# Moving the index load in front of the weights, re-ordering the start, and cutting loads and the last column finer, in a fused spectral-filter and gated-MLP kernel

## The chip, the cores and the metric

The kernel runs on one core of a Trainium2 chip. The time is that of one execution on the device, in microseconds (us); a profile gives a "span", which is about 1.7 us shorter than the time of the same execution (178.5 against 180.2 us). All executions below are with a granted TensorE clock of 0.996 to 1.0.

Engine names as in the profile: PE is TensorE (matmul), PEld its weight loads, DVE is VectorE, ACT is ScalarE, POOL is GpSimd, SP is the engine that issues the transfers (SPq: its queue).

## The reference, cut to what matters

```python
xn = _layernorm(x)                       # x: 2048 x 512, per row
A  = irfft2(rfft2(xn) * (w_r + 1j*w_i))  # spectral filter over both axes
g, u = xn @ w_gate, xn @ w_up            # 512 -> 1792
B  = (gelu(g) * u) @ w_down              # 1792 -> 512
return x + A + B
```

The 2048 rows are cut into 16 "columns" of 128 rows. A unit is a group of columns times some of the 14 blocks of 128 hidden features: its gate product goes through gelu on ACT (`ge`), DVE multiplies it with the up product (`hT`).

## The kernel before

The kernel records every operation with an estimated duration, and a planner orders them engine by engine. The order is fixed when the kernel is built; each engine then works through its list in turn. So a wrong estimate is not mended at run time: an engine stands in front of its next instruction until that one can start (1.66 us in one case below). The parts that matter here:

```python
# loads, all on one queue, in this order
load_x(0, 1)
load_x(1, 1)
for f0, f1 in ((0, 512), (512, 1024)):
    load_w(Wg_sb, f0, f1)
    load_w(Wu_sb, f0, f1)
    if f0 == 0:
        load_x(2, 2)
load_x(4, 4)
# ... third weight part, x 8-11, RF, x 12-15, constants ...
idx_t = pc.tile([P, 3], I32, name="idx_t")     # 128 rows of 12 bytes
nc.sync.dma_start(out=idx_t[:], in_=nc.inline_tensor(idx_np, name="spec_rows").ap())

# columns 2 and 3: moments, rsqrt in eight small DVE steps, normalise, transpose on PE, copy back
def second_two():
    m = [moments(c, -1200 + c) for c in (2, 3)]
    steps = rsqrt_steps(V, 2, 2)
    m = [add("DVE", 1.5, lambda: [f() for f in steps], m, key=-1190)]
    for c in (2, 3):
        xn_op[c] = add("DVE", 0.33, lambda c=c: f_norm_v(c, 0, D), m, key=-1180 + c, lat=0.53)
        # ... transpose and copy ...

# the first units: (first column, columns, first feature block, blocks)
todo = [(0, 1, 0, 2), (0, 1, 2, 2), (1, 1, 0, 4), (0, 2, 4, 2), (0, 2, 6, 2)]

# forward transform, four groups; each takes all four PSUM buffers "S" that ACT then copies out
def forward(cg, kv):
    # ...
    for q in range(4):
        m = pe(0.224, lambda q=q: mm(q), [f], 10 * cg + q, acq=("S",), rel=("xf",) if q == 3 else ())
        m.t_min = RF_LAND
        bs_ops.append(add("ACT", 0.5, lambda q=q: out(q), [m], key=10 + cg + 0.1 * q, rel=("S",)))

# output of column c; the last column in two halves
w = D if c < NC - 1 else D // 2
for o in range(0, D, w):
    # ... 14 matmuls, one more, DVE add, store ...
```

Between the warm-up matmuls and the first gate matmul PE runs six filler matmuls (`spin_on`), meant to keep its clock up.

## Time and profile before

| | before |
|---|---|
| time | 180.41 us, median of 3 (180.31 to 180.52) |
| span of the profiled execution | 178.5 us |
| PE busy | 172.8 us (97%) |
| DVE / ACT / POOL busy | 117.0 / 95.9 / 19.6 us |
| first gate matmul | 6.78 us |
| PE idle between that and the last matmul | 0.20 + 0.38 + 0.37 us |

First the head of the page: the span, PE's busy line and its strip of 40 slices.

```profile
span 178.5 us, 3086 instructions
...
PE   7999999999999999999999999999999999999992
```

PE is full everywhere but in the first and the last slice, so only the start, a few holes too short for the strip, and the tail can give time. The timeline of PE shows the start. Columns: start, length, engine, source line, operation, output and inputs, shape, count; in brackets the idle time in front and who ended it.

```profile
5.87 1.07 PE L318 MATMUL sp_ps<-x_t,spin 128*128 128x256 bf16 x6
6.78 0.61 PE L495 MATMUL g_ps<-xnT,Wg_sb 128*128 128x128 bf16 x8
...
8.10 1.07 PE L495 MATMUL u_ps<-xnT,Wu_sb 128*128 128x128 bf16 x16
9.00 1.06 PE L495 MATMUL g_ps<-xnT,Wg_sb 128*128 128x128 bf16 x16
10.27 1.05 PE L495 MATMUL g_ps<-xnT,Wg_sb 128*128 128x256 bf16 x8 [0.21 <-DMA Wg_sb<-in_B_w_gate_dram]
11.15 1.06 PE L495 MATMUL u_ps<-xnT,Wu_sb 128*128 128x128 bf16 x16
...
15.14 0.61 PE L495 MATMUL g_ps<-xnT,Wg_sb 128*128 128x256 bf16 x4
```

The eight matmuls at 10.27 need the second part of the gate weights, which landed at 10.22; the block before it issued its last matmul at 9.84 and the next could have started 0.05 later, so the hole is 0.38 us from start to start (the bracket counts from a modelled end). At 15.14 the first unit of columns 2 and 3 begins; this instant, called "gate block 2-3" below, closes the head, since PE runs without a wait from there to 40 us.

The one hole further on is in the forward transform. These are PE's timeline lines of the second and the third group:

```profile
35.98 1.06 PE L565 MATMUL bp<-RF_t,xf 128*128 128x128 bf16 x16
39.47 1.42 PE L565 MATMUL bp<-RF_t,xf 128*128 128x128 bf16 x16
```

And these are ACT's timeline lines between them; `Bs` are the copies out of PSUM, the memory that PE writes to; they free the buffers:

```profile
37.22 0.81 ACT L458 ACTIVATE xn<-x_t,nb,rstd 128x512 bf16<-128x512 bf16 x1 [1.66 <-POOL nb L373]
37.94 0.57 ACT L500 ACTIVATE ge<-g_ps 128x512 bf16<-128x512 f32 x1
38.42 2.04 ACT L535 CAST Bs<-bp 128x512 bf16<-128x512 f32 x4
```

Both groups on PE are 16 matmuls, but the second takes 1.42 us instead of 1.06: its tiles wait for these buffers. ACT could have copied out the group of 35.98 from about 36.4 on, but it stood 1.66 us in front of a normalisation that waited for POOL, and the copies came after it. The hole on PE is 0.37 us.

The tail, in DVE's timeline: the last add, after which only the store is left.

```profile
175.17 0.42 DVE L811 TENSOR_TENSOR y_sb<-y_ps,y_sb 128x256 bf16<-128x256 f32 x1 [0.73 <-PE y_ps L808]
```

### The profile page before, as it was taken

The page shows a single profiled execution, that of the slowest core. Times are in us where ns is not written, and L with a number is a line of the kernel's source. Part 1 is how long each engine was busy: PE and PEld are TensorE (multiplying, and loading weights), DVE is VectorE, ACT ScalarE, POOL GpSimd, SP SyncE. Part 2 cuts the span into 40 slices and gives each one's busy share as a digit, 9 for nine tenths or more (in the row PEclk, how much of TensorE's full clock was granted, in tenths as well). Part 3 has the DMA queues.
Part 4 walks back from the last instruction along what each step waited for, and adds up shares of the span by engine and source line. Part 5 has one row for each costly group of instructions (what it writes and reads, how often), then busy time and mean ns, then how long its engine had stood idle before and what let it go on. Part 6 is the DMA issues. An engine that isn't in the chain of part 4 may idle for free.

```text
span 178.5 us, 3086 instructions
## 1 busy us (share of the span) xinstructions
PE 172.8 (97%) x1100; PEld 95.7 (54%) x1118; DVE 117.0 (66%) x261; ACT 95.9 (54%) x172; POOL 19.6 (11%) x60
## 2 busy tenths in 40 slices
PE   7999999999999999999999999999999999999992
PEld 5688845464455544555555454454454445445461
DVE  3498999983843599979899999643616425334341
ACT  4633487969675988898899964362112112111200
POOL 1000363620576000000000000000000000000000
PEclk9999999999999999999999999999999999999999
DMA  4999944333392662211201520200122212222211
GB/s 117 350 384 393 371 130 95 79 63 32 70 296 106 217 200 59 56 26 37 54 23 44 130 69 15 59 0 0 62 88 88 90 59 62 90 87 63 84 33 59
DMA packets 21008, 19.36 MB, mean 108 GB/s; under 512 B 8128, under 2 KB 19520, under 8 KB 20992
## 3 DMA queue, kind: packets, MB, share of 16 engines
q1 hardware_dynamic: 20576, 17.84, 33.9%
q0 software_dynamic: 416, 1.32, 2.3%
q8 instruction: 9, 0.15, 0.3%
q14 instruction: 7, 0.06, 0.1%
HBM read 13.38 MB, written 2.10 MB: 87 GB/s over the span
## 4 chain that ended last, share of the span: by engine, by line
PE 90%; DMA 4%; ACT 2%; SPq 1%; issue 1%; DVE 1%
PE y_ps L804 27%; PE u_ps L495 26%; PE g_ps L495 25%; DMA Wg_sb<-in_B_w_gate_dram 4%; PE yp L756 2%; PE gp L726 2%; PE dp L623 2%; PE y_ps L808 2%; PE ep L632 2%; PE bp L565 1%; ACT Bs L535 1%; SPq L271 1%; ACT ge L500 1%; SPq L275 1%; DVE hT L505 0%
## 5 line engine op out<-in xcount | busy, mean ns | idle before, releaser
L495 PE MATMUL g_ps<-xnT,Wg_sb 128*128 128x512 bf16 (+2 forms) x268 | 57.1, 341 | 0.5 <-DMA Wg_sb<-in_B_w_gate_dram 0.2
L495 PE MATMUL u_ps<-xnT,Wu_sb 128*128 128x512 bf16 (+2 forms) x264 | 56.4, 340 | 0.3
L505 DVE TENSOR_TENSOR hT<-u_ps,ge 128x512 bf16<-128x512 f32 (+1 forms) x57 | 38.6, 678 | 19.3 <-PE u_ps L495 12.3
L804 PE MATMUL y_ps<-Wd_sb,hT 128*128 128x512 bf16 (+1 forms) x232 | 50.5, 366 | 0.3
L500 ACT ACTIVATE ge<-g_ps 128x512 bf16<-128x512 f32 (+1 forms) x57 | 34.1, 598 | 24.4 <-PE g_ps L495 23.0
L495 PEld LDWEIGHTS <-Wg_sb 128*128 128x128 bf16 x272 | 24.9, 98 | 21.5 <-DMA Wg_sb<-in_B_w_gate_dram 0.4
L495 PEld LDWEIGHTS <-Wu_sb 128*128 128x128 bf16 x272 | 24.8, 98 | 20.7 <-DMA Wu_sb<-in_B_w_up_dram 0.2
L804 PEld LDWEIGHTS <-hT 128*128 128x128 bf16 x238 | 22.9, 98 | 22.6
L762 ACT CAST yf<-yp 128x512 bf16<-128x512 f32 x16 | 9.3, 586 | 40.5 <-PE yp L756 40.5
L811 DVE TENSOR_TENSOR y_sb<-y_ps,y_sb 128x512 bf16<-128x512 f32 (+1 forms) x17 | 11.0, 659 | 30.2 <-PE y_ps L808 30.2
L637 ACT CAST E<-ep 64x512 bf16<-64x512 f32 x32 | 18.5, 578 | 0.9 <-PE ep L632 0.5
L333 DVE BATCH_NORM_STATS2 stats<-x_t 128x6 f32<-128x512 bf16 x16 | 10.4, 677 | 4.2 <-DMA x_t<-in_A_x_dram 4.0
L458 ACT ACTIVATE xn<-x_t,nb,rstd 128x512 bf16<-128x512 bf16 x12 | 9.8, 834 | 2.8 <-POOL nb L373 2.8
L535 ACT CAST ds<-dp 128x512 bf16<-128x512 f32 x16 | 9.2, 597 | 0.6 <-PE dp L623 0.5
L535 ACT CAST Gs<-gp 128x512 bf16<-128x512 f32 x16 | 8.7, 591 | 0.6 <-PE gp L726 0.5
L535 ACT CAST Bs<-bp 128x512 bf16<-128x512 f32 x16 | 8.5, 611 | 0.0
L768 DVE TENSOR_TENSOR lv<-yf 128x512 bf16<-128x512 bf16 x16 | 6.1, 421 | 1.5 <-ACT yf L762 0.7
L756 PEld LDWEIGHTS <-Gs 128*128 128x128 bf16 x64 | 4.8, 98 | 3.5
L775 DVE TENSOR_TENSOR yt<-lv 128x512 bf16<-128x512 bf16 x16 | 6.1, 421 | 0.3
L756 PE MATMUL yp<-CT,Gs 128*128 128x128 bf16 x64 | 6.0, 219 | 0.1
L808 PE MATMUL y_ps<-yt,RI_t 128*128 128x512 bf16 (+1 forms) x17 | 5.9, 366 | 0.0
L632 PE MATMUL ep<-ds,CT 128*128 128x512 bf16 x16 | 5.9, 379 | 0.0
(72 smaller groups left out, 121.5 us busy)
## 6 DMA issues: line engine op xcount, KB each, us to landing
F<-F SPq DMA_DIRECT2D x32, 64.0 KB, 2.0
y_sb<-in_A_x_dram SPq DMA_DIRECT2D x16, 128.0 KB, 2.1
out_dram<-y_sb SPq DMA_DIRECT2D x15, 128.0 KB, 1.7
Wd_sb<-in_B_w_down_dram SPq DMA_DIRECT2D x1, 1792.0 KB, 7.6
x_t<-in_A_x_dram SPq DMA_DIRECT2D x3, 512.0 KB, 11.5
Wg_sb<-in_B_w_gate_dram SPq DMA_DIRECT2D x2, 512.0 KB, 5.9
Wu_sb<-in_B_w_up_dram SPq DMA_DIRECT2D x2, 512.0 KB, 6.9
Wg_sb<-in_B_w_gate_dram SPq DMA_DIRECT2D x1, 768.0 KB, 9.4
```

The costliest lines, as they stand in the source:

```text
L333: V.bn_stats(out=st[:], in_=x_t[:, c, :])
L458: xn_op[c] = add("ACT", 0.72, lambda c=c: A.activation(out=xn[:, c, :], in_=x_t[:, c, :], func=AF.Identity, bias=nb[:, c:c + 1], scale=rst ...
L495: T_.matmul(b[name][:, f], lhsT=W_[:, e, (f0 + f) * P:(f0 + f + 1) * P], rhs=rhs[:, e, :], start=(e == 0), stop=(e == NE - 1))
L500: A.activation(out=b["ge"][:], in_=b["g_ps"][:], func=AF.Gelu_apprx_tanh)
L505: V.tensor_tensor(out=hT_of(sb, f0, m, o, w), in0=b["u_ps"][:], in1=b["ge"][:], op=ALU.mult)
L535: A.copy(out=o, in_=i)
L632: T_.matmul(t[:], lhsT=cc("L" if g + h else "L0"), rhs=b["ds", h][:], start=True, stop=True)
L637: A.copy(out=b["E"][64 * h:64 * h + 64, r], in_=b["ep", h][64 * r:64 * r + 64])
L756: T_.matmul(t[:, q], lhsT=late["G"][:, q, c0 + j], rhs=IQ[q], start=(q == 0), stop=(q == 3), skip_group_check=True)
L804: T_.matmul(b[o][:], lhsT=hT_of(sb, f, 1, cl * P, P)[:, 0], rhs=Wd_sb[:, f, o:o + w], start=(f == 0), stop=False)
L808: T_.matmul(b[o][:], lhsT=late["RI"][:, c, :], rhs=late["yt"][:, c, o:o + w], start=False, stop=True)
L811: V.tensor_tensor(out=b["y"][:, o:o + w], in0=b[o][:], in1=b["y"][:, o:o + w], op=ALU.add)
```

## The change

Its intent, as the code tells it: let column 1 land without weights behind it, order the start so that PE meets the loads later than they land, keep the small rsqrt steps of columns 2-3 together, shorten the last add and store. The diff, cut to its core (renamed variables and unchanged context left out):

```diff
     load_x(1, 1)
-    for f0, f1 in ((0, 512), (512, 1024)):
-        load_w(Wg_sb, f0, f1)
-        load_w(Wu_sb, f0, f1)
-        if f0 == 0:
-            load_x(2, 2)
-    load_x(4, 4)
+    idx_t = pc.tile([P, 3], I32, name="idx_t")
+    nc.sync.dma_start(out=idx_t[:], in_=nc.inline_tensor(idx_np, name="spec_rows").ap())
+    load_w(Wg_sb, 0, 512)
+    load_w(Wu_sb, 0, 512)
+    load_x(2, 2)
+    load_w(Wg_sb, 512, 1024)
+    load_w(Wu_sb, 512, 1024)
+    load_x(4, 2)
+    load_x(6, 2)
     ...                                  # x 8-11 and 12-15, RF and the constants in two each
-    LAND = {0: 2.9, 1: 3.8, 2: 7.9, 3: 7.9}
+    LAND = {0: 2.9, 1: 3.5, 2: 8.8, 3: 8.8}
-    WG_LAND = [5.6] * 4 + [9.3] * 4 + [15.0] * 6
-    WU_LAND = [7.0] * 4 + [10.8] * 4 + [17.0] * 6
+    WG_LAND = [6.6] * 4 + [10.2] * 4 + [15.0] * 6
+    WU_LAND = [8.0] * 4 + [11.7] * 4 + [17.0] * 6
     ...
         stats(1)
-        mean(1)
         recip(0)
         xn_(0, 0)
+        mean(1)
         xn_(0, 1)
-        recip(1)
     ...                                  # recip(1) after column 0's copies
+        hold[0] = m[0]                   # hT of unit 0 not before the rsqrt steps
+            hold[1] = xn_op[c]           # hT of unit 1 not before the normalisation
     ...
+        u = split("u_ps", "U", Wu_sb, 1000.5 + k, WU_LAND, 1 if k == 2 else m)
-    todo = [(0, 1, 0, 2), (0, 1, 2, 2), (1, 1, 0, 4), (0, 2, 4, 2), (0, 2, 6, 2)]
+    todo = [(0, 1, 0, 4), (1, 1, 0, 4), (0, 2, 4, 2), (0, 2, 6, 2)]
     ...
-        w = D if c < NC - 1 else D // 2
-        for o in range(0, D, w):
+        for o, w in ((0, D),) if c < NC - 1 else ((0, 256), (256, 128), (384, 128)):
```

`LAND` and its kin are the planner's estimates of when a load has landed; changing them changes the order, not the loads. On the queue five loads are cut in two, and the last store is.

More of the change, by code (lines that the diff above doesn't have):

```diff
@@ L280 @@
     load_x(1, 1)
-    for f0, f1 in ((0, 512), (512, 1024)):
-        load_w(Wg_sb, f0, f1)
-        load_w(Wu_sb, f0, f1)
-        if f0 == 0:
-            load_x(2, 2)
-    load_x(4, 4)
+    idx_t = pc.tile([P, 3], I32, name="idx_t")
[7 more added lines that the diff above has]
+    load_x(6, 2)
     load_w(Wg_sb, 1024, DF)
     load_w(Wu_sb, 1024, DF)
-    load_x(8, 4)
-    nc.sync.dma_start(out=RF_t[:], in_=rf_d.rearrange("p (c k) -> p c k", c=NC))
-    load_x(12, 4)
-    load_consts("F0", "M0")
-    LAND = {0: 2.9, 1: 3.8, 2: 7.9, 3: 7.9}
+    load_x(8, 2)
+    load_x(10, 2)
+    for c in range(0, NC, 8):
+        nc.sync.dma_start(out=RF_t[:, c:c + 8], in_=rf_d.rearrange("p (c k) -> p c k", c=NC)[:, c:c + 8])
+    load_x(12, 2)
+    load_x(14, 2)
+    load_consts("F0", "L0")
+    load_consts("I0", "M0")
+    LAND = {0: 2.9, 1: 3.5, 2: 8.8, 3: 8.8}
     LAND.update({c: 12.6 if c < 8 else 18.5 if c < 12 else 21.5 for c in range(4, NC)})
-    WG_LAND = [5.6] * 4 + [9.3] * 4 + [15.0] * 6
-    WU_LAND = [7.0] * 4 + [10.8] * 4 + [17.0] * 6
+    WG_LAND = [6.6] * 4 + [10.2] * 4 + [15.0] * 6
+    WU_LAND = [8.0] * 4 + [11.7] * 4 + [17.0] * 6
     RF_LAND = 20.0
-    idx_t = pc.tile([P, 3], I32, name="idx_t")
-    nc.sync.dma_start(out=idx_t[:], in_=nc.inline_tensor(idx_np, name="spec_rows").ap())
     for T, w_in in ((TR, A_w_r), (TI, A_w_i)):
@@ L427, in first_two @@
         copy(0, 1)
+        recip(1)
         v("xn1", lambda: f_norm_v(1, 0, D), 0.33, [("rstd", 1)], lat=0.45)
@@ L438, in moments @@
         return add("DVE", 0.1, lambda: f_mean(c), [s], key=key - 0.5)
+    hold = {}
     def second_two():
@@ L489, in unit, with mm @@
         rhs = xnT[sb][:, :, c0 % 4:c0 % 4 + n, :].rearrange("p e c q -> p e (c q)")
-        def mm(name, tag, W_):
-            b[name] = ps.tile([P, m, w], F32, name=name, tag=tag, bufs=2)
-            for f in range(m):
+        def mm(name, tag, W_, fs=range(m)):
+            if fs[0] == 0:
+                b[name] = ps.tile([P, m, w], F32, name=name, tag=tag, bufs=2)
+            for f in fs:
                 for e in range(NE):
@@ L508, in unit, with split @@
         src = [xT_op[c] for c in range(c0, c0 + n)]
-        g = add("PE", occ, lambda: mm("g_ps", "G", Wg_sb), src, key=1000 + k, lat=occ + 0.3, acq=("G",),
-                t_min=WG_LAND[f0 + m - 1])
-        u = add("PE", occ, lambda: mm("u_ps", "U", Wu_sb), src, key=1000.5 + k, lat=occ + 0.3, acq=("U",),
-                t_min=WU_LAND[f0 + m - 1])
+        def split(name, tag, W_, key, t, h):
+            o = None
+            for f in range(0, m, h):
+                o = add("PE", occ * h / m, lambda f=f: mm(name, tag, W_, range(f, f + h)), [o] if f else src, key=key,
+                        lat=occ * h / m + 0.3, acq=() if f else (tag,), t_min=t[f0 + f + h - 1])
+            return o
+        g = split("g_ps", "G", Wg_sb, 1000 + k, WG_LAND, 2 if k == 0 else m)
+        u = split("u_ps", "U", Wu_sb, 1000.5 + k, WU_LAND, 1 if k == 2 else m)
         ge = add("ACT", {1: 0.28, 2: 0.36, 4: 0.5}[n * m], f_ge, [g], key=-1000 + k,
                  lat={1: 0.38, 2: 0.48, 4: 0.7}[n * m], acq=("ge",), rel=("G",))
-        h = add("DVE", {1: 0.21, 2: 0.34, 4: 0.61}[n * m], f_h, [ge, u], key=-1000 + k, rel=("U", "ge"))
+        h = add("DVE", {1: 0.21, 2: 0.34, 4: 0.61}[n * m], f_h, [ge, u], key=-1000 + k, rel=("U", "ge"),
+                after=hold.get(k))
         for c in range(c0, c0 + n):
@@ L816, in down @@
         x = add("SP", 0.36, load, key=1000 + c, lat=2.6, acq=("y_sb",), t_min=100.0)
-        w = D if c < NC - 1 else D // 2
-        for o in range(0, D, w):
+        for o, w in ((0, D),) if c < NC - 1 else ((0, 256), (256, 128), (384, 128)):
             k = 2000 + 10 * c + o / D
-            m = add("PE", 14 * w * 0.000421, lambda o=o: mm(o, w), [h_op[c, f] for f in range(NFC)] + [wd],
+            m = add("PE", 14 * w * 0.000421, lambda o=o, w=w: mm(o, w), [h_op[c, f] for f in range(NFC)] + [wd],
                     key=k, acq=("S",))
-            r = add("PE", w * 0.000421, lambda o=o: ri_mm(o, w), [m, yt_op[c], ri], key=k + 0.1,
+            r = add("PE", w * 0.000421, lambda o=o, w=w: ri_mm(o, w), [m, yt_op[c], ri], key=k + 0.1,
                     lat=w * 0.000421 + 0.3)
             m.lat = m.occ
-            t = add("DVE", 0.1 + w * 0.001, lambda o=o: total(o, w), [r, x], key=k, rel=("S",))
-            add("SP", 0.36, lambda o=o: store(o, w), [t], key=k, lat=2.0, rel=("y_sb",) if o + w == D else ())
+            t = add("DVE", 0.1 + w * 0.001, lambda o=o, w=w: total(o, w), [r, x], key=k, rel=("S",))
+            add("SP", 0.36, lambda o=o, w=w: store(o, w), [t], key=k, lat=2.0, rel=("y_sb",) if o + w == D else ())
     for c in range(NC):
```

## The prediction

> **What bounds it now.** TensorE. In the timeline, matmuls follow each other without a gap from 10.27 us to 175.1 us of the 178.5 us span (PE busy 97%, granted clock 1.0 throughout). The only holes after the first gate matmul at 6.78 us: 0.20 us before 8.10 (first up weights), 0.38 before 10.27 (the chain of waits blames the second gate load, issued 3.27, landed 10.22), and 0.37 inside the third forward-transform group (40.0 to 40.5), whose PSUM buffers ScalarE freed late because it sat 1.66 us in order behind GpSimd (37.22). About 0.95 us in all. After the last matmul: VectorE add 0.42, store 1.6 to landing, 1.3 to the end. Only the head, these holes and the tail can give anything; no matmul column is removed.
>
> **What the change does.**
> 1. The index load goes in front of the weights. Its issue takes 0.33 us (timeline), plus about 0.05. Column 1 then has a tiny transfer, not 512 KB of weights, behind it: landed at 4.00, it should land near 3.5. The weights are issued about 0.37 later, and I expect loads to land 0.2 to 0.4 later: first gate 6.64 to about 6.95, up 8.05 to 8.35, columns 2-3 8.74 to 9.05, second gate 10.22 to 10.5.
> 2. Column 0's chain shortens (column 1's mean moved behind): copies end near 6.0 instead of 6.4. That buys nothing: the first gate matmul waits for weights, near 7.0 instead of 6.78.
> 3. Column 1's 16 up matmuls (0.87 us) now come before the second gate block, so the 0.38 us hole closes.
> 4. The rsqrt steps of columns 2-3 run unbroken (about 1.6 us), but the first hT multiply (0.69) sits between them and the normalisation. I reckon stats 9.1, scale 12.2, xn 12.9 to 13.6: PE may wait 0.2 to 0.4 us at the third up tile and the transposes. The gate block of columns 2-3, at 15.14 now, starts between 14.8 and 15.4: head worth -0.3 to +0.3 us.
> 5. Split loads move the same bytes; the queue is bandwidth-bound at 360 to 415 GB/s until about 22 us: nothing on the critical path.
> 6. Re-planned order: the second and third forward groups move about 2 units back, so the 0.37 us hole probably closes.
> 7. Tail: from adds of 0.69 (512 columns) and 0.42 (256) I estimate 0.29 for 128, saving 0.13 us. PE time is equal (128-wide matmuls already run at 54 ns). The Trainium skill, "DMA: Bandwidth & Descriptors" (Anatomy of one DMA), puts the fixed part near 2.0 us; here whole stores take 1.7 and halves 1.6, so halving again gains 0 to 0.05. The same page (Specifications) says transfers below 512 B are not line-rate, and these rows are 256 B: a small risk of the opposite sign. No run here shows it yet.
>
> **Sum.** Head about 0, forward hole -0.3, tail -0.15: from 180.41 to **180.0 us**, 8 in 10 between **179.3 and 180.7**. Faster by over 2%: 0.01; within 2%: 0.98; slower by over 2%: 0.01.
>
> **What would show it.** Column 1 landing near 3.5; first gate matmul near 7.0, no wait for the second gate load; gate block of columns 2-3 at 15.1 +- 0.3; no stall over 0.1 us in the forward groups; last add near 0.29 us, last store landing in about 1.6.
>
> **What would make it wrong.** The index load not delaying the weights (0.3 more gain); its 12-byte rows blocking queues longer than one issue (loss); a new in-order stall of ScalarE behind GpSimd or the late table load; 256-byte stores landing slower than 2 us.

## The result, and the profile after

The change took the time from 180.45 us (180.31 to 180.52) to 179.38 us (179.14 to 179.73), four runs each. The ratio is 0.9943, 95% interval 0.9922 to 0.9964. Ratios here are the mean time of one kernel's runs over that of the other's of the same rounds, so not quite the ratio of the medians quoted. A second series, of five runs (whether on the same chip is not on record), gave 179.21 us against 179.81 for before, ratio 0.9971 (0.9958 to 0.9984). The gain is thus 0.5 to 1.1 us. The two series differ mainly in the kernel before: all its four runs of the first series lie above 180.3 us, and the profiled execution (180.2) had late loads (below). Why it was slower there is not shown. The forecast of 180.0, range 179.3 to 180.7, held the result near its lower edge.

First the head of the page again, span and PE's strip:

```profile
span 177.5 us, 3118 instructions
...
PE   7999999998999999999999999999999999999993
```

The 8 in the tenth slice (40 to 44 us) is the larger hole shown below.

PE's timeline at the start, to be held against the one of before:

```profile
5.69 0.82 PE L323 MATMUL sp_ps<-x_t,spin 128*128 128x256 bf16 x6
6.34 0.61 PE L505 MATMUL g_ps<-xnT,Wg_sb 128*128 128x128 bf16 x8
...
7.79 1.07 PE L505 MATMUL u_ps<-xnT,Wu_sb 128*128 128x128 bf16 x16
8.69 1.06 PE L505 MATMUL g_ps<-xnT,Wg_sb 128*128 128x128 bf16 x16
9.59 1.06 PE L505 MATMUL u_ps<-xnT,Wu_sb 128*128 128x128 bf16 x16
10.48 1.91 PE L505 MATMUL g_ps<-xnT,Wg_sb 128*128 128x256 bf16 x16
12.23 0.60 PE L505 MATMUL u_ps<-xnT,Wu_sb 128*128 128x256 bf16 x4
12.66 0.61 PE L350 MATMUL tp<-ident_t,xn 128*128 128x128 bf16 x8
...
14.42 1.04 PE L505 MATMUL g_ps<-xnT,Wg_sb 128*128 128x256 bf16 x8
```

Column 1's up matmuls now stand at 9.59, in front of the block that needs the second gate load, and the hole before that block is gone. In front of the first up matmuls, which need weights landed at 7.74, PE stands 0.30 us instead of 0.20. Gate block 2-3 starts at 14.42 instead of 15.14, although PE has done the same matmuls by then. The other hole is still there, and larger. PE's lines of the second and third group:

```profile
36.11 1.06 PE L581 MATMUL bp<-RF_t,xf 128*128 128x128 bf16 x16
...
39.60 0.83 PE L581 MATMUL bp<-RF_t,xf 128*128 128x128 bf16 x12
...
40.88 0.38 PE L581 MATMUL bp<-RF_t,xf 128*128 128x128 bf16 x4 [0.45 <-ACT Bs L551]
```

ACT's lines over the same stretch:

```profile
36.41 0.81 ACT L467 ACTIVATE xn<-x_t,nb,rstd 128x512 bf16<-128x512 bf16 x1 [0.92 <-POOL nb L378]
37.13 0.58 ACT L510 ACTIVATE ge<-g_ps 128x512 bf16<-128x512 f32 x1
37.60 0.80 ACT L467 ACTIVATE xn<-x_t,nb,rstd 128x512 bf16<-128x512 bf16 x1
38.31 1.55 ACT L551 CAST Bs<-bp 128x512 bf16<-128x512 f32 x3
39.73 0.62 ACT L510 ACTIVATE ge<-g_ps 128x512 bf16<-128x512 f32 x1
40.22 0.61 ACT L551 CAST Bs<-bp 128x512 bf16<-128x512 f32 x1
```

ACT waits less for POOL (0.92 instead of 1.66 us), but the new order puts a second normalisation (37.60) and a gelu (39.73) between the four copies, so the last buffer is free at 40.83, and the group's last four matmuls wait for it: 0.61 us from start to start beyond the usual 0.055. The tail, DVE's timeline again:

```profile
174.72 0.29 DVE L827 TENSOR_TENSOR y_sb<-y_ps,y_sb 128x128 bf16<-128x128 f32 x1 [0.55 <-PE y_ps L824]
```

To see where the span went I cut it at four instants that both traces have. A second profile of each kernel, taken with the experiments, stands beside the first:

| us | before | before, again | after | after, again |
|---|---|---|---|---|
| start to gate block 2-3 | 15.14 | 14.78 | 14.42 | 14.33 |
| from there to the start of the last matmul | 159.72 | 159.70 | 160.04 | 160.02 |
| from there to the landing of the last store | 2.35 | 2.36 | 2.09 | 2.09 |
| from there to the end | 1.29 | 1.29 | 0.92 | 0.92 |
| span | 178.50 | 178.13 | 177.47 | 177.37 |

The last three lines repeat to 0.02 us; the first does not. The first profile of before was an execution with late loads: its first gate load landed at 6.64 us, that of the second profile, issued at the same 1.71, at 5.75. Between the two second profiles the change gains 0.45 us in the head (a third profile with the loads and order of before, that of the six-more run below, has 14.64 there, which would leave 0.2 to 0.3), loses 0.32 in the middle (0.24 of it the larger hole, 0.05 because a 128-wide last matmul starts later than a 256-wide one), gains 0.27 up to the landing, and 0.37 in a place where no engine computes.

### The profile page after: what moved, and what is told of

Read it like the earlier page. It is cut to its first block, busy times and chain, and to the rows that moved or that the text cites. A ratio compares the mean times of both kernels' runs of the same rounds, so it can differ in the third digit from the quotient of the medians.

```text
span 177.5 us, 3118 instructions
## 1 busy us (share of the span) xinstructions
PE 172.1 (97%) x1115; PEld 96.0 (54%) x1133; DVE 116.6 (66%) x261; ACT 96.5 (54%) x171; POOL 20.1 (11%) x60
## 4 chain that ended last, share of the span: by engine, by line
PE 83%; ACT 5%; DMA 3%; issue 3%; POOL 2%; DVE 1%; SPq 1%; ACTq 0%
PE y_ps L820 27%; PE u_ps L505 23%; PE g_ps L505 22%; DMA Wu_sb<-in_B_w_up_dram 3%; PE dp L639 2%; ACT Bs L551 2%; PE yp L772 2%; PE gp L742 2%; PE y_ps L824 2%; PE ep L648 2%; ACT xn L467 2%; ACT ge L510 1%; DVE hT L515 1%; PE bp L581 1%; POOL t L366 0%
## 5 line engine op out<-in xcount | busy, mean ns | idle before, releaser
L505 PE MATMUL g_ps<-xnT,Wg_sb 128*128 128x512 bf16 (+2 forms) x265 | 56.4, 340 | 0.4
L515 DVE TENSOR_TENSOR hT<-u_ps,ge 128x512 bf16<-128x512 f32 x56 | 38.5, 688 | 19.0 <-PE u_ps L505 10.5
L820 PE MATMUL y_ps<-Wd_sb,hT 128*128 128x512 bf16 (+2 forms) x246 | 50.6, 355 | 0.3
L510 ACT ACTIVATE ge<-g_ps 128x512 bf16<-128x512 f32 x56 | 33.9, 606 | 21.4 <-PE g_ps L505 17.6
L827 DVE TENSOR_TENSOR y_sb<-y_ps,y_sb 128x512 bf16<-128x512 f32 (+2 forms) x18 | 11.1, 631 | 30.0 <-PE y_ps L824 30.0
L824 PE MATMUL y_ps<-yt,RI_t 128*128 128x512 bf16 (+2 forms) x18 | 6.1, 355 | 0.0
L742 PEld LDWEIGHTS <-F 128*128 128x128 bf16 x64 | 4.5, 98 | 2.6
```

The costliest lines, as they stand in the source:

```text
L505: T_.matmul(b[name][:, f], lhsT=W_[:, e, (f0 + f) * P:(f0 + f + 1) * P], rhs=rhs[:, e, :], start=(e == 0), stop=(e == NE - 1))
L510: A.activation(out=b["ge"][:], in_=b["g_ps"][:], func=AF.Gelu_apprx_tanh)
L515: V.tensor_tensor(out=hT_of(sb, f0, m, o, w), in0=b["u_ps"][:], in1=b["ge"][:], op=ALU.mult)
L820: T_.matmul(b[o][:], lhsT=hT_of(sb, f, 1, cl * P, P)[:, 0], rhs=Wd_sb[:, f, o:o + w], start=(f == 0), stop=False)
L824: T_.matmul(b[o][:], lhsT=late["RI"][:, c, :], rhs=late["yt"][:, c, o:o + w], start=False, stop=True)
L827: V.tensor_tensor(out=b["y"][:, o:o + w], in0=b[o][:], in1=b["y"][:, o:o + w], op=ALU.add)
```

## The experiments

The theory after the result: the head gained by order, the index load costs something, the middle lost to the hole, the last 0.37 us came from the number of transfers. Each part has a rival, told in the expectations. Every batch ran on one chip with its own runs of before, so ratios are to that before: medians 179.81, 179.93 and 179.89 us, 11 runs each. Experiments are compared across chips by these ratios.

### 1. The control, and the index load put back

The changed kernel once more:

> The changed kernel once more, as the control of this batch and a second sample of its load landings. If the early landing of the weights (first gate 6.27 us, first up 7.74, spread of one load over its 16 engines about 0.6 us) comes from the index load in front, it shows again within 0.1 us; if it was luck of one execution, some landing moves by 0.3 us or more. Time 179.2 to 179.7.

And with the index load behind the constants:

```diff
     load_x(1, 1)
-    idx_t = pc.tile([P, 3], I32, name="idx_t")
-    nc.sync.dma_start(out=idx_t[:], in_=nc.inline_tensor(idx_np, name="spec_rows").ap())
     load_w(Wg_sb, 0, 512)
     ...
+    idx_t = ...                          # after the constants
```

> The changed kernel with the index load back behind the constants; the number of transfers and every other engine's order are the same. Theory A (the small load between column 1 and the weights makes the weights land earlier although they are issued 0.47 us later): first gate load lands near 6.64 again, first up near 8.05, with a spread near 1.3 us; TensorE starts the first up tile near 8.1 instead of 7.79, and the time rises by 0.2 to 0.4 us. Rival B (the landing does not depend on it, the head was gained by order alone): landings near 6.3 and 7.7 or, issued 0.47 earlier, near 5.9 and 7.3; time equal or 0.1 to 0.3 lower.

The opposite edit, the index load moved forward in the kernel before:

> The kernel before with only the index load moved between column 1 and the weights. Theory A (spacer): first gate lands near 6.3, first up near 7.75, columns 2-3 near 8.4, second gate near 10.1, spread about 0.6 us; the order of before can use little of it, as its first gate matmul waits for the fillers until 6.78 and its second gate block starts at the landing: time 0.1 to 0.3 us lower. Rival B: everything lands 0.3 to 0.5 later (7.0, 8.4, 9.1, 10.6), time 0.3 us higher.

Measured: the control 179.21 us (ratio 0.9971), index late 179.00 us (0.9953, 0.9942 to 0.9965), before with index early 180.38 us (1.0029, 1.0016 to 1.0042). My theory A was wrong: the index load in front does not bring the weights earlier. The control alone could not tell, as it repeated the first profile's landings to 0.12 us (6.15 and 7.65), about as theory A asked; the two moves of the index load could. This table of the traces collects all 14 profiles, seven with the index load late, seven with it early (median, and range):

| landed at, us | index late | index early |
|---|---|---|
| column 1 | 3.73 (3.40 to 4.00) | 3.42 (3.41 to 3.67) |
| first gate part | 5.82 (5.71 to 6.64) | 6.15 (5.98 to 6.27) |
| first up part | 7.38 (7.18 to 8.05) | 7.67 (7.60 to 7.74) |
| second gate part | 9.89 (9.72 to 10.22) | 10.13 (9.89 to 10.62) |

The spacer does what the prediction said: column 1 lands 0.3 us earlier and the weights about 0.3 us later, having been issued 0.47 us later. The ranges overlap, because a load counts as landed only with the last of its 16 semaphore counts, and that one scatters (for the first gate load it comes 0.4 to 1.4 us after the first); the first count of that load comes at 5.17 to 5.29 us with the index late and at 5.47 to 5.71 with it early, so the shift is clear. For the kernel before, which waits on the second gate load, that is a loss of 0.52 us (0.0029 of 179.81). In the trace of before with the index early, PE's hole in front of the second gate part is 1.13 us. For the changed kernel a loss is not shown: the ratios differ by 0.3 us, but their intervals just overlap, and the profiles show none. With the index late, PE starts the first up matmuls at 7.42 instead of the control's 7.70, but then stands 0.47 us in front of the third up tile, from 11.86 to 12.33, until DVE's first hT multiply, held behind the rsqrt steps, has freed its buffer at 12.27. Gate block 2-3 starts at 14.52, later than the control's 14.33. The early weights of the changed kernel's first profile, which had suggested theory A, were an ordinary execution beside a late one of before.

### 2. The number of transfers

One constants load cut in two, nothing else, in the changed kernel:

```diff
     load_consts("F0", "L0")
-    load_consts("I0", "M0")
+    load_consts("I0", "I3")
+    load_consts("M", "M0")
```

> The changed kernel with the last constants load cut in two, so one transfer more; nothing else moves. Theory A (at the end the queue engine polls its eight completion semaphores one by one, about 0.065 us each; in the changed kernel the last store has the eighth, so nothing is left to poll after it landed): the last store now has the first semaphore, seven polls follow its landing, and the time rises by about 0.4 us (0.3 to 0.5). Rival B (only bytes and landings count, the tail was gained by the smaller last store): no change, within 0.1 us.

Six transfers more in the kernel before, by cutting its one constants load into seven:

```diff
-    load_consts("F0", "M0")
+    for n0, n1 in (("F0", "F1"), ("F2", "F3"), ("L", "L0"), ("I0", "I1"), ("I2", "I3"), ("M", "M"), ("M0", "M0")):
+        load_consts(n0, n1)
```

> The kernel before with its one constants load cut into seven: six transfers more, as many as the changed kernel has, and nothing else. Theory A (the last store's place among the eight completion semaphores): the last store moves from the second to the eighth, no poll follows its landing, and the time falls by 0.3 to 0.45 us. Rival B (polls cost nothing that shows in the time): no change, or up to 0.2 us more for the extra issues.

Measured: one more 179.55 us against 179.21 of the control in the same batch (0.9989 against 0.9971, so +0.32 us, intervals just overlapping); six more 179.60 against 179.93 (0.9981, 0.9966 to 0.9996, so -0.34 us). The traces show the reason. The queue's transfers take eight completion semaphores in turn. After the last instruction the SP engine waits for all eight, one after another, in fixed order. The trace puts these waits at the line of kernel.py that opens the Tile context (L860 before, L875 after), so they are instructions of the program as it was built. Their ends, read from the raw trace (each record starts when its wait is over), in us:

```
                  last store landed   ends of the eight waits
before                  177.21        176.20 177.23 177.29 177.36 177.42 177.48 177.54 177.60
before, six more        176.62        175.47 175.54 175.60 175.67 175.73 175.79 175.85 176.64
after                   176.55        175.48 175.55 175.62 175.68 175.75 175.81 176.10 176.57
after, one more         176.43        176.44 176.51 176.58 176.64 176.70 176.76 176.82 176.88
```

In before the last store has the second semaphore: when it lands, six waits that were long satisfied still follow, about 0.062 us each. With six transfers more it has the eighth and nothing follows. With one more again it has the first and seven follow. Landing to end of span: 1.29, 0.92, 0.92 and 1.36 us. This is shown, not argued: the count was changed alone, in both directions, the traces show the waits moving with it, and the time followed, for six more clear of the noise.

### 3. The last column

```diff
-        for o, w in ((0, D),) if c < NC - 1 else ((0, 256), (256, 128), (384, 128)):
+        for o, w in ((0, D),) if c < NC - 1 else ((0, 256), (256, 256)):
```

with one constants transfer more, to keep the last store on the eighth semaphore.

> The changed kernel with its last column in 256 + 256 again, and one constants transfer more so that the count, and with it the last store's semaphore, stays. Theory: the last add takes 0.42 instead of 0.29 us and the store lands 0.08 later, so the time rises by 0.15 to 0.25 us against the changed kernel. Rival (the tail was gained by the semaphore alone): no rise, within 0.05 us.

Measured: 179.73 us (0.9988, 0.9969 to 1.0007), on another chip than the control (0.9971); the time alone does not decide 0.2 us. The trace does. The view of transfers shows the last stores of this kernel (number, KB each, median us from issue to landing):

```profile
out_dram<-y_sb SPq DMA_DIRECT2D x1, 128.0 KB, 1.7
out_dram<-y_sb SPq DMA_DIRECT2D x2, 64.0 KB, 1.6
```

and those of the changed kernel:

```profile
out_dram<-y_sb SPq DMA_DIRECT2D x1, 64.0 KB, 1.6
out_dram<-y_sb SPq DMA_DIRECT2D x2, 32.0 KB, 1.5
```

From the start of the last matmul to the landing it is 2.29 us here and 2.09 in the changed kernel; 0.05 of that is the later start of a narrower matmul. So the finer column is worth 0.15 us, nearly all of it the add (0.42 to 0.29). The kernel before has 2.35, so a further 0.06 of the tail's gain came without the finer column; the six-more run of before has 2.30, with its last store landing in 1.53 us instead of 1.59. Why the store is quicker there is open.

### 4. The hole in the third forward group

```diff
-            m.t_min = RF_LAND
+            m.t_min = 41.7 if cg == 2 else RF_LAND
```

This tells the planner that the third group may not start before 41.7 of its own clock; it then stands one gate and one up block later in PE's list.

> The changed kernel with the third forward group planned later, so that its four tiles find their PSUM buffers free. Theory (the hole of 0.6 us at 40.8 is a wait for ScalarE's copies of the second group, and TensorE is the limit behind it): the hole closes to under 0.1 us and the time falls by 0.4 to 0.6 us. Rival (something else would bind behind it, the fourth group or the first spectral groups): the hole reappears later and the time stays within 0.2 us.

Measured: 178.83 us (0.9938, 0.9921 to 0.9954). PE's line for the third group, where the changed kernel had two pieces with a gap:

```profile
41.28 1.06 PE L581 MATMUL bp<-RF_t,xf 128*128 128x128 bf16 x16
```

The 16 matmuls run in 1.06 us and no new hole follows: from gate block 2-3 to the last matmul it is 159.43 us instead of 160.02, 0.59 less, the whole hole. The theory held and its rival fell. (The planner also moved the fourth group forward, from 48.87 to 46.49; it runs without a hole in both places.)

### 5. The order alone, and the unbroken chain alone

The kernel before with only the new order (its loads, index place and last column kept):

> The kernel before with only the new order of TensorE, VectorE and ScalarE (column 1's mean later, the first unit in one piece, the unbroken rsqrt chain, the new load estimates of the planner); loads and last column as before. Theory (the order gives the head its gain and the third forward group its loss): no hole in front of the second gate block, the gate block of columns 2-3 starts 0.2 to 0.4 us earlier than before at equal landings, the hole at 40.8 is 0.6 instead of 0.36 us, and the time falls by 0 to 0.2 us. Rival (the order is worth most of the 0.6 to 1.0 us): it falls by over 0.4 us.

Measured: 179.79 us against 179.89 (0.9989, 0.9975 to 1.0002, so -0.2 us, an interval that includes zero). Its profiled execution had late loads (first gate part 6.50, second 10.13), close to those of the first profile of before (6.64, 10.22), which makes the two comparable: no hole before the second gate part, gate block 2-3 at 14.60 instead of 15.14, and a hole of 0.61 us in the third group instead of 0.37. So the order gives about 0.45 us in the head at similar, late loads (0.54 less the 0.09 by which the second gate load was earlier) and takes 0.24 back in the middle.

The changed kernel without the two `hold` lines:

```diff
-        hold[0] = m[0]
-            hold[1] = xn_op[c]
```

> The changed kernel without the rule that keeps the hT multiplies out of the rsqrt chain of columns 2-3; the planner then puts the first hT multiply in front of the chain, where before had it. Theory (that one multiply of 0.69 us only changes places with the chain, the normalisation comes at the same moment, so the unbroken chain is worth little): time within 0.15 us of the changed kernel, apart from what the planner moves in the forward groups. Rival (the unbroken chain is what the head gained): TensorE waits 0.3 us or more at the transposes of columns 2-3 and the time rises as much.

Measured: 180.63 us (180.04 to 181.25; 1.0051, 1.0031 to 1.0070). I had expected nothing and it is slower than the changed kernel by about 0.8% (the control ran on another chip), and slower than before in the same batch. The planner put one hT multiply in front of the rsqrt steps and another between them and the normalisation, and it moved the transposes on PE behind the third and fourth up tile. PE's timeline:

```profile
12.15 1.91 PE L503 MATMUL u_ps<-xnT,Wu_sb 128*128 128x256 bf16 x16
13.90 0.61 PE L350 MATMUL tp<-ident_t,xn 128*128 128x128 bf16 x8
15.25 0.50 PE L503 MATMUL g_ps<-xnT,Wg_sb 128*128 128x256 bf16 x3 [0.74 <-DVE xnT L353]
```

The transposes start at 13.90 instead of 12.66, no up tile is left on PE to cover the copies that follow, and gate block 2-3 waits until 15.25, 0.83 us later than in the changed kernel. So the theory that the multiply only changes places was wrong: the normalisation itself starts 0.63 us later (12.69 instead of 12.06; 0.17 of it because columns 2-3 landed at 8.59 instead of 8.42), and the transposes 1.24 later, because of their new place on PE. How much each of the two is worth was not tested apart. The profiled execution was the fastest of the six; why the others are up to 1.2 us slower still is open.

### 6. Two combinations

Index late and third group later:

> The changed kernel with the index load at its old late place and the third forward group planned later. If the two effects add (0.2 us from the index load, 0.5 us from the hole), it is 0.6 to 0.8 us faster than the changed kernel and 0.7 to 0.85 percent faster than before; if the earlier weights only run into the moment chain of columns 2-3 (a wait of 0.3 to 0.5 us at 12.3), the index load gives nothing more and it is near 178.8.

The same, with the first hT multiply allowed in front of the chain and the planner given the landings measured with the index late:

> As the run before, and in addition the first hT multiply is allowed in front of the rsqrt chain and the planner has the landings measured with the index load late. If the wait at 12.3 is for the PSUM buffer that this multiply frees after the chain, it goes, and the time is 0.2 to 0.4 us below the run before (178.3 to 178.6); if it is for the transposes, it only moves.

Measured: 178.73 us (0.9930, 0.9917 to 0.9943) and 178.99 us (0.9947, 0.9934 to 0.9960). The first is the fastest kernel, 1.2 us under before in the same batch, and every one of its runs is faster than every run of the changed kernel (on other chips); whether the late index adds anything to the closed hole (178.83 and 0.9938 with that alone, on another chip) is not decided. The wait in front of 12.33 us, seen with the index late, did not occur in its profile, where the multiply ended at 12.00 and PE came to that tile at 12.23; but there is a new hole of 0.23 us at 107.4, inside a `gp` group, and from gate block 2-3 to the last matmul it is 159.66 us, against 159.43 in experiment 4. The second did not help. Its profiled execution, the slowest of five, started the first gate matmul only at 7.18, though the weights were there at 5.82:

```profile
5.99 1.36 PE L323 MATMUL sp_ps<-x_t,spin 128*128 128x256 bf16 x6
...
7.18 1.06 PE L504 MATMUL g_ps<-xnT,Wg_sb 128*128 128x128 bf16 x16
```

Two things delayed it. Its column 0 had landed at 3.43 us, against 2.91 to 3.14 in the other 13 profiles, so the fillers began at 5.99 instead of 5.69. And the six fillers take 1.36 us here and 0.82 in the changed kernel: five of the six took 0.21 us each instead of 0.11, so PE still ran at half its later pace (the granted clock, 1.0 here too, does not show this). The Trainium skill, "TensorE: Matmul & The Clock Gate" (What's actually happening), says that the window which raises the clock is free-running and does not reset when a kernel starts; the traces fit this, in that the fillers run slow in four of 14 profiles and over different counts (three, two, three and five of six), the first profile of before among them. It is a second source, besides the landings, of the head's scatter.

## Why the prediction was right or wrong, point by point

- **What bounds it**: right. PE without holes, and the three places where it waits.
- **1, index load**: right in kind and size as to the landings. Column 1 at 3.42 by the median, 3.67 in the first profile (forecast 3.5), weights later by 0.3 (forecast 0.2 to 0.4). But the levels were taken from one execution of before in which all loads were late, so "first gate near 6.95" came out as 6.27. The experiments, not the first pair of profiles, showed this delay; that it costs time is shown for the kernel before alone.
- **2, column 0's shorter chain buys nothing**: half right. Its copies ended at 6.24 (forecast 6.0) and the first gate matmul at 6.34 (forecast 7.0), with weights at 6.27. Copies, weights and the fillers' end (the last was issued at 6.23) now meet.
- **3, hole before the second gate block closes**: right.
- **4, head worth -0.3 to +0.3 with a wait of 0.2 to 0.4 us at the transposes**: wrong. No such wait appeared in the first profile or the control (the wait itself is real: 0.14 us at the third up tile in the run of experiment 3, 0.47 with the index late), and gate block 2-3 came at 14.42, outside 14.8 to 15.4. The order is worth about -0.45 us at similar loads, against the "head about 0" of the sum. The mechanism was right; the term was mis-sized, because the sum added a delay of the loads to an execution that was already late: columns 2-3 landed at 8.42, forecast about 9.05.
- **5, split loads "nothing on the critical path"**: this step failed. Bytes were indeed not the matter, but the count was: -0.37 us, the semaphore of the last store. The profile's engines say nothing about it; the 1.3 us after the landing stood in the prediction as a constant, and it is none.
- **6, the forward hole closes**: wrong in sign. It grew from 0.37 to 0.61 us. The prediction looked at PE's list only; ACT's list, which can be read just as well before a run, shows the normalisation and the gelu between the copies.
- **7, tail**: right. Add 0.29 as estimated, store landed in 1.51 us. The Trainium skill, "DMA: Bandwidth & Descriptors" (Anatomy of one DMA), puts a fixed part near 2.0 us on a transfer, in a section on transfers issued by GpSimd; these stores are issued by SP, and here 128 KB ones take 1.7, 64 KB ones 1.5 to 1.6 and 32 KB ones 1.5 in all. The risk named from its section Specifications, that pieces under 512 B are read and written back, shows no cost in these stores with 256 B rows, though no run has stores of 32 KB with longer rows to hold against them.

Sum: forecast -0.4 us, measured -1.1 in the first series and -0.6 in the second. Between the two second profiles, the parts are -0.45 (head, index load included), +0.32 (middle), -0.27 (last matmul to landing), -0.37 (semaphore). The missed semaphore made up for the wrong sign of the hole; that the range held was partly luck.

Left open: the split loads by themselves, apart from their count, were not run, and neither was the changed kernel's head with the index late over several profiles. What the order, the last column and the semaphore do not explain between the kernel with the new order (0.9989) and the changed kernel with the index late (0.9953) is small: 0.65 us measured, 0.52 from semaphore and last column, and the two ran on different chips.

## What to carry to other kernels

Where one engine is full, read the ends too: which of a queue's completion semaphores the last store gets was worth more here (0.37 us) than halving that store (0.15 us), and it changes whenever any transfer is added or merged. In a plan fixed at build time, check the list of every engine around a shared buffer, because one in-order wait of an off-path engine (ACT behind POOL) opens a hole in the full one; moving the consumer back by two blocks closed 0.6 us. And take landing times from several executions before sizing anything under 1 us: one profile of the kernel before was late by 0.9 us in its first weights.

## What the Trainium skill lacked or had wrong

- "DMA: Bandwidth & Descriptors" lacks, and "Runtime: NRT & Kernel Launch" lists barriers and resets after a kernel without, what the end of this kernel's own program shows: after the last store the issuing engine waits for the eight completion semaphores of its transfers in fixed order, about 0.062 us each, so the end comes 0.92 us after the landing when the last store has the eighth, 1.29 with the second and 1.36 with the first.
- "DMA: Bandwidth & Descriptors" (Latency and other measured facts) gives an access latency by load, but no scatter of landings between executions: the same first gate load, issued at 1.71 us, landed between 5.71 and 6.64 us in seven profiles.
- "DMA: Bandwidth & Descriptors" (Specifications) states a penalty below 512 B; stores with 256 B rows landed in 1.51 us, those with 512 B rows in 1.53 to 1.61, so none is seen; but the 32 KB stores moved half the bytes of the others, so a penalty below about 0.1 us could hide (an estimate, from the 0.12 us between 128 and 64 KB stores).
- "ScalarE: Activation LUTs" (What ACT_TABLE_LOAD costs) adds a drain of about 1.38 us to the load of 1.28 us for every switch; no such drain is seen here. The load itself agrees (1.28 us). In the changed kernel it starts at 7.85, 0.01 us after ACT's copy ended (7.25 + 0.59), and the next activation starts at 9.14, so the switch cost 1.3 us in all.
